# Stage B of an FFT mixer moved from block-diagonal 128x128 matmuls to 64x64 array tiles, inside a fused mixer and gated FFN

## The chip, the cores and the metric

One core of a Trainium2 chip runs the whole kernel. The metric is the device time of one execution in microseconds; lower is better. Engines are named as in the profile: PE (matmul), PEld (weight load), DVE (VectorE), ACT (ScalarE), POOL (GpSimd), SP (the queue that issues most DMAs).

## The reference

```python
def _attn_ref(x, filt_r, filt_i):              # x: (8, 3008, 256)
    X = np.fft.rfft(x, axis=1)
    Y = X * (filt_r + 1j * filt_i)[None]       # 1505 frequencies x 256 channels
    return np.fft.irfft(Y, n=x.shape[1], axis=1)

def _moe_ref(x, w_gate, w_val, w_out):         # x: (24064, 256), d_ff = 1536
    return (np.maximum(x @ w_gate, 0.0) * (x @ w_val)) @ w_out
```

The output of the first function, reshaped to 24064 rows, is the input of the second.

## The kernel before, in words

The transform of length 3008 is factored as 94 x 32. For each of the 8 batches there are three stages:

- **Stage A** is the transform of length 94. Batches 0 and 1 take it in `items_a`: 16 items, each one fp32 matmul of 128x96 weights `WA` on 512 columns of `XF`, a copy by ACT, and a write to the DRAM buffer `Abuf` after every fourth item. Batches 2 to 7 take `load_chunk`, `fold_chunk` and `tiled_a`, four chunks per batch: six DMAs bring `x` into a buffer `XP`, POOL folds it with six additions and subtractions, and sixteen fp32 matmuls on 32x32 array tiles transform it.
- **Stage B** (`items_b`) reads `Abuf` back transposed as `at`. The 94 frequencies of stage A are 48 lines, held as 24 groups of two. For two groups at a time, `fwd` makes the 32-point transform: two matmuls of 256 columns with weights `F2[:, g]` into one PSUM bank `psX`. DVE multiplies the bank twice, with the real and the imaginary filter, into `tt` and `uu`. `inv` makes the inverse 32-point transform: four matmuls with `I2t` and `I2u`, accumulating in `psD`, which ACT copies to `dsb`; a DMA writes it to `Dbuf`. The weights of a group are block-diagonal 128x128 matrices, one 64x64 block for each of its two lines; the other half is zero.
- **Stage C** (`item_c`) reads `Dbuf` as `dC` and makes the inverse of length 94 so that its output is the FFN input `yT`, 512 tokens at a time.

The FFN runs over 47 blocks of 512 tokens, and each block over 12 steps. A step is `gv` (two matmuls of 512 columns for `psV`, two for `psG`; ACT copies `psV` to `vsb`, DVE makes relu(gate) times value) and `o_part` of the block before (four matmuls of 256 columns). The order of work is written by hand: `at_step(s, f)` hangs pieces of stages A and B and their DMAs on step numbers, and `side` is emptied after each step's matmuls. `item_c` of the next block follows at steps 8 and 10 of each block. Stage B of batches 1 to 7 hangs on every second step, as 12 pieces of `fwd` and `inv` and two more of `inv`.

Before step 0 stands a prologue: stage A of batch 0, the making of `I2t` and `I2u` from `F2` (`make_back`), loading of the filters, stage B of batch 0 with dummy matmuls (`warm`) and three items of A of batch 1 in between (`amid`), the other 13 items, and `item_c` of block 0. Six products of batch 0 go to POOL instead of DVE (`POOL_G`), for which ACT first copies the bank to `xs`.

PSUM is four tags of two banks each: `fft`, `psv`, `psg`, `pso`. In the prologue stages rotate over all four; afterwards `fft_tag` gives `fft` alone, so that stages B and C share its two banks.

Of the kernel before, what the change touches and what calls it, by code (L numbers as in the profile page):

```python
# [30 lines left out]
NROW = 96  # L31
# [10 lines left out]
def _tables():  # L42
# [3 lines left out]
    wa = np.zeros((128, NROW + 2))  # L46
    for a in range(2):
        wa[64 * a:64 * a + 64, NROW + a] = 1.0
# [7 lines left out]
    for hg in range(48):  # L56
        g, a = divmod(hg, 2)
        rows = slice(a * 64, a * 64 + 64)
        f = np.zeros((64, 64))
# [4 lines left out]
        wa[part, 2 * hg] = np.cos(th)  # L64
        if k1 not in (0, 47):
            wa[part, 2 * hg + 1] = -np.sin(th)
            m1[48 * a + g] = 2.0 * np.cos(th) / S
            m1[48 * a + 24 + g] = -2.0 * np.sin(th) / S
# [8 lines left out]
        else:  # L77
            m1[48 * a + g] = np.cos(th) / S
# [15 lines left out]
        f2[lo + 64 * a, g] = f  # L94
# [4 lines left out]
    col = 4 * (8 * (r % 4) + r // 4 % 8) + 2 * (r // 64) + r // 32 % 2  # L99
    perm = np.zeros((128, 128))  # L100
    perm[r, col] = 1.0
# [15 lines left out]
    tab = np.concatenate([f2.reshape(128, -1), perm, swap, own.reshape(128, -1), m1], 1)  # L117
    return wa.astype(np.float32), fold.reshape(128, 128).astype(np.float32), tab.astype(NBF16)
# [3 lines left out]
def kernel(  # L122
# [17 lines left out]
    NZ = 8  # L140
# [4 lines left out]
    wa_h, fold_h, tab_h = _tables()  # L145
# [14 lines left out]
    WA = pro.tile([128, NROW + 2], FP32)  # L160
    WF = consts.tile([128, 4, 32], FP32)
    M1 = consts.tile([NROW, N1], BF16)
    F2 = consts.tile([128, NG, 128], BF16)
    I2t = consts.tile([128, NG, 128], BF16)
    I2u = consts.tile([128, NG, 128], BF16)
# [20 lines left out]
    f2c = tabs[:, 0:NG * 64].rearrange("p (g f) -> p g f", f=64)  # L186
    perm, swap = tabs[:, NG * 64:NG * 64 + 128], tabs[:, NG * 64 + 128:NG * 64 + 256]

    def place_forward():
        for a in range(2):  # L190
            nc.vector.tensor_scalar(F2[:, :, a * 64:a * 64 + 64], f2c,
                                    WA[:, NROW + a:NROW + a + 1], None, op0=ALU.mult)
        nc.vector.tensor_copy(M1, tabs[:NROW, NG * 64 + 512:])

    def make_back(i, q):

        psI = ps.tile([128, 4, 128], FP32, tag=fft_tag(), name="psI")
        gs = slice(4 * q, 4 * q + 4)
        if i == 0:
            for j in range(4):  # L200
                nc.tensor.matmul(psI[:, j], F2[:, 4 * q + j, :], perm, start=True, stop=True)
        else:
            nc.tensor.matmul(psI, swap, I2t[:, gs, :], start=True, stop=True)
        copy = nc.scalar.copy if i == 1 else nc.vector.tensor_copy
        copy((I2t, I2u)[i][:, gs, :], psI)

    def place_own():

        for i, t in enumerate((I2t, I2u)):
            o = NG * 64 + 256 + i * 128  # L210
            nc.vector.tensor_copy(
                t[64:, NG - 2:, :].rearrange("p g (n a c) -> p g n a c", a=2, c=2)[:, :, :, 1, :],
                tabs[64:, o:o + 128].rearrange("p (g n c) -> p g n c", g=2, c=2))
# [50 lines left out]
    def fft_tag():  # L264
        turn["i"] += 1
        return turn["tags"][turn["i"] % len(turn["tags"])]

    def items_a(b):

        def one(c, j, st):  # L270
            if j == 0:
                st["asb"] = sb.tile([128, NC2 * D], BF16, tag="asb", bufs=4, name="asb")
            psA = ps.tile([128, 512], FP32, tag=fft_tag(), name="psA")
            o = (c * NC2 % NX2) * D + j * 512
            nc.tensor.matmul(psA[0:NROW], WA[:, :NROW], XF[c * NC2 // NX2][:, o:o + 512],  # L275
# [13 lines left out]
    def load_chunk(b, j):  # L289

        xp = XP[(4 * b + j) % 3]
        for q in range(4):
            r, o = 32 * q, 8 * q + 2 * j
            nc.sync.dma_start(xp[r:r + 24, 0:4:2, :],
                              _ap(x, (b * N1 * N2 + o) * D,
                                  [[N2 * D, 24], [47 * N2 * D, 2], [1, 512]]))
        for i in range(2):
            nc.sync.dma_start(xp[:, 2 * i + 1, :],
                              _ap(x, ((b * N1 + 46 + 47 * i) * N2 + 2 * j) * D,
                                  [[8 * D, 4], [-N2 * D, 32], [1, 512]]))  # L300

    def fold_chunk(b, j):

        xp = XP[(4 * b + j) % 3]
# [29 lines left out]
    def load_at_tiled(b):  # L334

        ats[b] = sb.tile([128, NG, D], BF16, tag="at", bufs=1, name="at")
        for rr in range(4):
            for e in range(2):
                nc.sync.dma_start(ats[b][32 * rr:32 * rr + 32, e:NG:2, :],
                                  _ap(Abuf[b], (48 * (rr % 2) + 24 * e + 12 * (rr // 2)) * N2 * D,  # L340
                                      [[D, 32], [N2 * D, 12], [1, D]]))

    GC = 6
    POOL_G = (4, 6, 10, 12, 16, 18)
# [8 lines left out]
    def items_b(b, amid=None):  # L353

        held = []
        st = {}
        lag = 2 if b else 3
        cuts = (0, 6, 12, 18, 24) if b else (0, 6, 12, 18, 22, 24)

        def fwd(g):  # L360
            at = ats[b]
            psX = ps.tile([128, 2, D], FP32, tag=fft_tag(), name="psX")
            for i in range(2):
                nc.tensor.matmul(psX[:, i], F2[:, g + i, :], at[:, g + i, :], start=True, stop=True)  # L364
            tt = sb.tile([128, 2, D], BF16, tag="tt", bufs=4)
            uu = sb.tile([128, 2, D], BF16, tag="uu", bufs=4)
            nc.vector.tensor_tensor(tt, psX, Ftr[:, g:g + 2, :], op=ALU.mult)  # L367
            if b == 0 and g in POOL_G:
                xs = pro.tile([128, 2, D], FP32, tag="xs", bufs=2)
                nc.scalar.copy(xs, psX)  # L370
                nc.gpsimd.tensor_tensor(uu, xs, Fti[:, g:g + 2, :], op=ALU.mult)  # L371
            else:
                nc.vector.tensor_tensor(uu, psX, Fti[:, g:g + 2, :], op=ALU.mult)  # L373
            held.append((g, tt, uu))

        def inv():
            g, tt, uu = held.pop(0)
            if g in cuts:
                st["dsb"] = sb.tile([128, GC, D], BF16, tag="dsb", bufs=4, name="dsb")
                st["g"] = g  # L380
            psD = ps.tile([128, 2, D], FP32, tag=fft_tag(), name="psD")
            for i in range(2):
                nc.tensor.matmul(psD[:, i], I2t[:, g + i, :], tt[:, i], start=True, stop=False)  # L383
                nc.tensor.matmul(psD[:, i], I2u[:, g + i, :], uu[:, i], start=False, stop=True)  # L384
            o = g - st["g"]
            nc.scalar.copy(st["dsb"][:, o:o + 2, :], psD)  # L386
            if g + 2 in cuts:
                nc.sync.dma_start(_ap(Dbuf[b], st["g"] * D, [[NG * D, 128], [1, (o + 2) * D]]),
                                  st["dsb"][:, :o + 2, :])

        for g in range(0, NG, 2):
            def both(g=g):
                fwd(g)
                if amid:
                    amid(g // 2)
                if len(held) > lag:
                    inv()
            yield both
        for _ in range(lag):
            yield inv  # L400
# [3 lines left out]
    def load_d(b, z0=0, z1=NZ):  # L404
        for z in range(z0, z1):
            dC = sb.tile([NROW, 4, D], BF16, tag="dC", bufs=12)
            nc.sync.dma_start(dC, _ap(Dbuf[b], z * 4 * NROW * D,
# [225 lines left out]
```

## Time and profile before

| what | value |
|---|---|
| median of 3 runs | 913.89 us (913.39 to 914.81) |
| the profiled execution's own time | 913.1 us |
| its span, first to last instruction | 911.3 us |
| PE busy / DVE / ACT / POOL | 98% / 63% / 55% / 29% |
| mean granted PE clock | 0.995 |

The span runs from the first to the last instruction of the core; 1.8 us of the execution lie around it. "Busy" of PE counts pipelined matmuls until their modelled end, so spacing between the starts of matmuls says more than their durations: a matmul of 512 columns is listed with 379 ns and the next one starts 216 ns after it.

### The profile page before, as it was taken

The numbers are of one execution on the slowest core, as the hardware profiler recorded it, in microseconds if no ns is written. First come the engines' busy times: TensorE is split into PE (matmuls) and PEld (weight loads), VectorE is DVE, ScalarE is ACT, GpSimd is POOL, SyncE is SP. The second block draws the span as 40 slices with busy tenths as digits, with TensorE's granted clock in tenths as the row PEclk, the third lists the DMA queues.
The fourth block names the chain that finished last, engine by engine and source line by source line (L and its number), as shares of the span: only waits on it lengthen the run. The fifth ranks groups of instructions, "written<-read, shape, count | busy, mean of one in ns | idle before, by whom it ended". The sixth has DMA issues, their size and how long they took to land.

```text
span 911.3 us, 18044 instructions
## 1 busy us (share of the span) xinstructions
PE 896.0 (98%) x6602; PEld 545.7 (60%) x6602; DVE 578.0 (63%) x875; ACT 500.8 (55%) x893; POOL 262.4 (29%) x181
## 2 busy tenths in 40 slices
PE   8799999999999999999999999999999999999997
PEld 3445665666655666556655566556665566666665
DVE  3737766568655775657755587555865567655553
ACT  4675555555555555555555555555555555555552
POOL 4340174405451074400844017440355300000000
PEclk9899999999999999999999999999999999999999
DMA  9996336444355345452353433525446242231111
GB/s 254 256 252 143 116 122 166 111 90 138 122 153 105 82 150 139 119 117 84 129 168 94 115 111 118 165 76 121 115 134 166 65 106 66 85 78 36 36 31 51
DMA packets 106138, 109.04 MB, mean 120 GB/s; under 512 B 9794, under 2 KB 87362, under 8 KB 105410
## 3 DMA queue, kind: packets, MB, share of 16 engines
q1 hardware_dynamic: 101222, 103.77, 40.7%
q0 software_dynamic: 4512, 3.90, 2.8%
q8 instruction: 52, 0.85, 0.4%
q14 instruction: 36, 0.29, 0.1%
q10 hardware_dynamic: 316, 0.22, 0.1%
HBM read 61.94 MB, written 49.81 MB: 123 GB/s over the span
## 4 chain that ended last, share of the span: by engine, by line
PE 95%; DMA 3%; SPq 0%; ACT 0%; POOL 0%; DVE 0%; issue 0%; ACTq 0%; POOLq 0%
PE psV L445 27%; PE psG L445 27%; PE psO L464 26%; PE psF L321 3%; PE psA L275 3%; PE psY L429 2%; PE psD L383 2%; PE psD L384 2%; PE psX L364 2%; DMA XF<-in_x_dram 1%; DMA Abuf<-asb 1%; DMA at<-Abuf 0%; DMA out_dram<-osb 0%; SPq L178 0%; SPq L478 0%
## 5 line engine op out<-in xcount | busy, mean ns | idle before, releaser
L450 DVE SCALAR_TENSOR_TENSOR prod<-psG,vsb 128x512 bf16<-128x512 f32 x564 | 390.0, 692 | 274.6 <-ACT vsb L448 265.6
L448 ACT CAST vsb<-psV 128x512 bf16<-128x512 f32 x564 | 332.0, 589 | 244.7 <-PE psV L445 206.4
L445 PE MATMUL psV<-yT,WvT 128*128 128x512 bf16 x1128 | 335.9, 379 | 0.9 <-ACT yT L434 0.7
L464 PE MATMUL psO<-WoT,prod 128*128 128x256 bf16 x2256 | 336.4, 273 | 0.0
L445 PE MATMUL psG<-yT,WgT 128*128 128x512 bf16 x1128 | 335.3, 379 | 0.0
L464 PEld LDWEIGHTS <-prod 128*128 128x128 bf16 x2256 | 220.7, 98 | 143.4
L445 PEld LDWEIGHTS <-WgT 128*128 128x128 bf16 x1128 | 110.0, 98 | 133.8 <-issue 0.5
L307 POOL TENSOR_TENSOR fold<-XP 128x1024 f32<-128x1024 f32 x24 | 56.4, 2351 | 404.5 <-DMA out_dram<-osb 170.9
L445 PEld LDWEIGHTS <-WvT 128*128 128x128 bf16 x1128 | 102.3, 98 | 33.1 <-issue 20.9
L386 ACT CAST dsb<-psD 128x512 bf16<-128x512 f32 x96 | 55.9, 588 | 51.7 <-PE psD L384 50.0
L367 DVE TENSOR_TENSOR tt<-psX,Ftr 128x512 bf16<-128x512 f32 x96 | 65.2, 682 | 4.2 <-PE psX L364 4.2
L470 ACT COPY osb<-psO 128x512 f32<-128x512 f32 x92 | 53.9, 586 | 22.7 <-PE psO L464 20.3
L373 DVE TENSOR_TENSOR uu<-psX,Fti 128x512 bf16<-128x512 f32 x90 | 61.3, 681 | 0.0
L308 POOL TENSOR_TENSOR XP<-XP 128x1024 f32<-128x1024 f32 x24 | 56.4, 2349 | 1.9
L384 PE MATMUL psD<-uu,I2u 128*128 128x256 bf16 x192 | 47.6, 276 | 0.6 <-POOL uu L371 0.6
L383 PE MATMUL psD<-tt,I2t 128*128 128x256 bf16 x192 | 47.9, 276 | 0.0
L328 ACT CAST asb<-psF 128x512 bf16<-128x512 f32 x48 | 25.8, 589 | 32.5 <-PE psF L321 32.5
L328 DVE CAST asb<-psF 128x512 bf16<-128x512 f32 x48 | 30.9, 686 | 17.3 <-PE psF L321 14.5
L364 PE MATMUL psX<-at,F 128*128 128x256 bf16 x192 | 37.8, 281 | 3.9 <-DMA at<-Abuf 3.9
L436 DVE CAST yT<-psY 128x512 bf16<-128x512 f32 x47 | 32.0, 681 | 12.9 <-PE psY L429 12.9
L434 ACT CAST yT<-psY 128x512 bf16<-128x512 f32 x47 | 27.5, 586 | 22.7 <-PE psY L429 22.6
L429 PE MATMUL psY<-M,dC 96*128 96x94 bf16 (+18 forms) x604 | 37.5, 198 | 0.0
(64 smaller groups left out, 439.9 us busy)
## 6 DMA issues: line engine op xcount, KB each, us to landing
dC<-Dbuf SPq DMA_DIRECT2D x64, 192.0 KB
XP<-in_x_dram SPq DMA_DIRECT2D x48, 256.0 KB
Dbuf<-dsb SPq DMA_DIRECT2D x31, 384.0 KB
XP<-in_x_dram SPq DMA_DIRECT2D x96, 96.0 KB
Abuf<-asb SPq DMA_DIRECT2D x96, 96.0 KB
at<-Abuf SPq DMA_DIRECT2D x48, 192.0 KB
out_dram<-osb SPq DMA_DIRECT2D x70, 94.0 KB
XF<-in_x_dram SPq DMA_DIRECT2D x12, 256.0 KB
```

Source lines behind the costliest of these rows:

```text
L307: tt(t, xp[:, 0:2], xp[:, 2:4], op=ALU.add)
L308: tt(xp[:, 2:4], xp[:, 0:2], xp[:, 2:4], op=ALU.subtract)
L328: copy(asf[:, :, q, :], banks[q])
L364: nc.tensor.matmul(psX[:, i], F2[:, g + i, :], at[:, g + i, :], start=True, stop=True)
L367: nc.vector.tensor_tensor(tt, psX, Ftr[:, g:g + 2, :], op=ALU.mult)
L373: nc.vector.tensor_tensor(uu, psX, Fti[:, g:g + 2, :], op=ALU.mult)
L383: nc.tensor.matmul(psD[:, i], I2t[:, g + i, :], tt[:, i], start=True, stop=False)
L384: nc.tensor.matmul(psD[:, i], I2u[:, g + i, :], uu[:, i], start=False, stop=True)
L445: nc.tensor.matmul(pt[:, :W], w[:, h, ft * 128:(ft + 1) * 128], yt[:, h, :], start=(h == 0), stop=(h == 1))
L448: nc.scalar.copy(vsb, psV[:, :W])
L450: nc.vector.scalar_tensor_tensor(prod, in0=psG[:, :W], scalar=0.0, in1=vsb, op0=ALU.max, op1=ALU.mult)
L464: nc.tensor.matmul(psO[:, t % 2], prods[ft][:, t * 128:(t + 1) * 128], WoT[:, ft, :], start=(ft == 0), stop=(ft == NFT - 1))
```

## The change

Five things are done.

1. Stage B is issued on 64x64 array tiles. `fwd(b, i)` takes four groups at a time with eight matmuls of 64x64 weights (`tile_position=(64*e, 64*a)`), into two PSUM banks, one for each row half `e`. `inv(b, i)` takes sixteen matmuls into two banks `psD`. A batch needs six of each. `F2`, `I2t`, `I2u` hold 64 columns per group instead of 128, `F2` comes straight by DMA, and `make_back_t`/`make_back_u` are three calls each, of which the first uses 64x64 tiles too.
2. For batches 1 to 7 stage B stands at seven steps in place of fourteen, "excursions" here: the first has a `fwd`, five have a `fwd` and the `inv` of the excursion before, the last has an `inv`. The four products of an excursion stand on four steps in a row. `psX` takes both `fft` banks; `psD` takes one bank of `psv` and one of `psg`.
3. Stage B of batch 0 is six excursions; seven of its 24 products go to POOL. After excursion 2 one item of A of batch 1 follows, after each of 3, 4 and 5 two, in banks of `pso`; nine are left for afterwards. `x` of batch 1 is loaded in smaller first pieces.
4. The `x` chunks of batches 2 to 7 are loaded by POOL's queue, one per FFN block, each held until `yT` of the next block is being made; the folding of a chunk follows the load of the next.
5. `dC` tiles hold eight rows in place of four (half as many, two DMAs each), `load_at_tiled` takes four DMAs in place of eight, `XP` has four buffers, `osb` four in place of five, and `dsb` is written in three pieces for each batch in place of four.

```diff
-    for i in range(2):
-        nc.tensor.matmul(psX[:, i], F2[:, g + i, :], at[:, g + i, :], start=True, stop=True)
...
+def fwd(b, i):
+    for e in range(2):
+        psXs[b, i, e] = ps.tile([128, 2, D], FP32, tag=fft_tag(), name="psX")
+    for m in range(2):
+        for e in range(2):
+            for a in range(2):
+                j = 12 * a + 2 * i + m
+                nc.tensor.matmul(psXs[b, i, e][64 * a:64 * a + 64, m],
+                                 F2[64 * e:64 * e + 64, j, :],
+                                 ats[b][64 * e:64 * e + 64, j, :], start=True, stop=True,
+                                 tile_position=(64 * e, 64 * a))
...
+def product(b, i, e, k, pool=False):
+    psX = psXs[b, i, e]
...
+    if pool:
+        xs = pro.tile([128, 2, D], FP32, tag="xs", bufs=3)
+        nc.scalar.copy(xs, psX)
+        nc.gpsimd.tensor_tensor(p, xs, filt, op=ALU.mult)
+    else:
+        nc.vector.tensor_tensor(p, psX, filt, op=ALU.mult)
...
+def inv(b, i, tags=None, cuts=CUTS):
...
+    for m in range(2):
+        for k in range(2):
+            for a in range(2):
+                for e in range(2):
+                    nc.tensor.matmul(psD[a][64 * e:64 * e + 64, m],
+                                     (I2t, I2u)[k][64 * a:64 * a + 64, 4 * i + 2 * m + e, :],
+                                     tus[b, i, e, k][64 * a:64 * a + 64, m],
+                                     start=(k == 0), stop=(k == 1),
+                                     tile_position=(64 * a, 64 * e))
...
+def first_b(amid):
+    cuts = (0, 2, 4, 5, 6)
+    for i in range(6):
+        fwd(0, i)
+        if i > 1:
+            inv(0, i - 2, cuts=cuts)
+        for e in range(2):
+            product(0, i, e, 0)
+            product(0, i, e, 1, pool=(i, e) in POOL_U)
+        amid(i)
+    inv(0, 4, cuts=cuts)
+    inv(0, 5, cuts=cuts)
...
-        xp = XP[(4 * b + j) % 3]
+        xp = XP[j]
...
-            nc.sync.dma_start(xp[r:r + 24, 0:4:2, :],
+            nc.gpsimd.dma_start(xp[r:r + 24, 0:4:2, :],
...
-    load_x(1, nc.sync, WHOLE)
+    load_x(1, nc.sync, ((0, 0, 2 * q), (0, 2 * q, 4 * q), (1, 0, 4 * q)))
...
 def amid(i):
-    if i < 9:
-        warm(1, 128)
+    if i < 2:
+        warm(3, 256)
     else:
-        next(early)()
+        for _ in range(2 if i > 2 else 1):
+            next(early)()
...
-    load_d(0, 0, 2)
+    load_d(0, 0, 1)
...
-        sb0 = 19 if b == 1 else end - 30 | 1
...
+            for j, e in enumerate((-74, -69, -64, -57)):
+                l = end - 113 + NFT * j
+                def next_x(b=b, j=j, l=l):
+                    hold_gpsimd(yTs[l // NFT + 1][:, 0, 0:8])
+                    load_chunk(b, j)
+                    if j:
+                        fold_chunk(b, j - 1)
+                    if j == 3:
+                        fold_chunk(b, j)
+                at_step(l, next_x)
+                at_step(end + e, lambda b=b, j=j: tiled_a(b, j))
+            at_step(end + e + 4, lambda b=b: load_at_tiled(b))
+        for i, l in enumerate((-35, -28, -25, -22, -16, -11, -4) if b == 1 else
+                              (-40, -35, -28, -23, -16, -11, -4)):
+            if i < 6:
+                at_step(end + l, lambda b=b, i=i: fwd(b, i))
+                for h in range(4):
+                    at_step(end + l + h, lambda b=b, i=i, h=h: product(b, i, h // 2, h % 2))
+            if i > 0:
+                at_step(end + l, lambda b=b, i=i: inv(b, i - 1, ("psv", "psg")))
+        at_step(end - 2, lambda b=b: load_d(b))
```

Here `end` is `(b * S // W - 1) * NFT + C_AT[0] - 5`: step 51 for batch 1 and 72 steps more for each further batch.

## The prediction

> **What bounds it now.** First the page's busy times and the chain that ended last:
>
> ```profile
> PE 896.0 (98%) x6602; PEld 545.7 (60%) x6602; DVE 578.0 (63%) x875; ACT 500.8 (55%) x893; POOL 262.4 (29%) x181
> PE 95%; DMA 3%; SPq 0%; ACT 0%; POOL 0%; DVE 0%; issue 0%; ACTq 0%; POOLq 0%
> ```
>
> PE carries the chain. Busy shares overstate a pipelined engine, so next the PE timeline, where only starts count:
>
> ```profile
> 47.68 0.27 PE L383 MATMUL psD<-tt,I2t 128*128 128x256 bf16 x1
> 47.79 0.27 PE L384 MATMUL psD<-uu,I2u 128*128 128x256 bf16 x1
> 47.90 0.27 PE L383 MATMUL psD<-tt,I2t 128*128 128x256 bf16 x1
> ```
>
> Listed as 0.27 us, they start 0.11 apart (0.109 in the trace's records). Between 61.9 and 905.8 us I added up all starts: L445 keeps 0.216, L464 and stage B's L364, L383, L384 keep 0.109 all through, and the only losses are one start 0.63 us late at 73 us and the entries into and exits from L321. Hence in the FFN part **every matmul slot taken away is time**, and a wait only costs if PE feels it. An FFN step is 4 x 0.216 + 4 x 0.109 = 1.30 us.
>
> How array tiles behave is seen at `tiled_a`:
>
> ```profile
> 135.37 0.60 PE L464 MATMUL psO<-WoT,prod 128*128 128x256 bf16 x4
> 135.90 0.61 PE L321 MATMUL psF<-XP,WF 24*32 24x512 f32 x1
> ...
> 136.04 0.62 PE L321 MATMUL psF<-fold,WF 24*32 24x512 f32 x2
> ...
> 136.64 0.59 PE L321 MATMUL psF<-XP,WF 24*32 24x512 f32 x1
> 137.16 0.39 PE L445 MATMUL psV<-yT,WvT 128*128 128x512 bf16 x1
> ```
>
> and in the weight loads there:
>
> ```profile
> 136.06 0.11 PEld L321 LDWEIGHTS psF<-fold,WF 24*32 24x32 f32 x2
> ```
>
> The last L464 starts at 135.37 + 3 x 0.109 = 135.70 and L321 follows 0.20 later, 0.09 over its slot. After the last L321 (512 fp32 columns in two passes of 0.43, as L275 shows) PE goes on after 0.52, again 0.09 over. One pass of sixteen tiles to the next takes about 0.46, so tiles run side by side; and the load at 136.06 is for the second pass of tiles whose first pass started at 136.04, so a load hides under a running matmul of its own tile. The whole takes 1.26 us, of which 2 x 0.43 are work, 0.09 the exit and 0.31 a stagger: the third and fourth row start 0.13 and 0.27 late, behind semaphore instructions for their banks.
>
> Last, the prologue:
>
> ```profile
> 43.75 1.07 PE L275 MATMUL psA<-XF,WA 128*96 128x512 f32 x2 [1.54 <-DMA XF<-in_x_dram]
> 49.43 11.32 PE L275 MATMUL psA<-XF,WA 128*96 128x512 f32 x26
> 60.59 0.61 PE L429 MATMUL psY<-M,dC 96*128 96x94 bf16 x11
> 53.14 1.67 SPq L407 DMA_DIRECT2D dC<-Dbuf x2
> ```
>
> PE waits for `x` of batch 1 and then has 11 us of stage A before `psY`; but the second `dC` that `psY` needs lands only at about 60.4 us by its semaphore, so the DMA chain is as long as PE's.
>
> **What the Trainium skill says.** "TensorEngine Tiling (Array Packing)", Tiling Modes, Key Properties: a change of tiling mode drains the engine. The trace agrees, 0.09 in and 0.09 out. The same page, Tile-to-Partition Mapping, Restrictions: column tiling switches the fast weight load off. No 64-column bf16 load is in this trace. "TensorE: Matmul & The Clock Gate", Part 3, The mechanism: a load overlaps running matmuls only where its row group differs. The 136.06 row speaks against it; the measurement decides. "DMA: Bandwidth & Descriptors", Issuing engines are not separate DMA queues: another issuing engine saves only issue time; no run here shows it.
>
> **Stage B, batches 1 to 7.** Removed: per batch 24 matmuls of L364 and 48 of L383/L384, 72 x 0.109 = 7.85 us, 54.9 in all. Added: 48 + 96 matmuls on 64x64 tiles. Four tiles run side by side, so 36 packs of four; a pack of 256 columns is taken at 0.109, from L364. That gives 3.92 per batch, 27.5 in all. Mode changes: 7 excursions x 7 batches x 0.18 = 9.0. Waits inside an excursion: `fwd` and `inv` each open two banks, so the second half of the tiles starts behind its semaphore instruction; tiled_a's stagger of 0.31 is the ceiling, nothing (hidden behind running packs) the floor, and I take 0.15: 49 x 0.15 = 7.4. Sum 43.9 against 54.9, **-11.0**. A pack's own bounds are 0.109 and 0.13 (the 0.46 against 0.43 of a tiled_a pass, with room), up to +5.
>
> **DVE and ACT around it.** Products and `dsb` copies keep their number and shape. Backlogged products start 0.60 apart (34.59, 35.19, 35.79 for L373 and L367), so a step of STT (0.69) and one product costs DVE 1.30: it just keeps pace for four steps, and the excursion ahead of them (about 1 us without STT) gives slack. ACT gets two `psD` copies of 0.59 at once; the next `vsb` is then some 0.8 late, and the two buffers of `psv` and `psg` hide that, since they are needed again a step later. I cost both at nothing for batches 2 to 7, where excursions are five or more steps apart. **Batch 1** has them at steps 23, 26 and 29: the fourth product of one stands on the very step whose `fwd` wants its bank. There STT and that product (0.69 + 0.65) run while PE waits, with `gv` of the next step behind it: 1.35 x 2 = **+2.7**. Its `at` loads move from step 5 to 3 and the first `fwd` from 19 to 16; the last part landed at 77.9 us before, 1.7 us earlier now, and step 16's `fwd` stands near 80.
>
> **Queues.** Per chunk six DMAs go from SP to POOL. POOL then has, at the fourth chunk, six issues of about 0.6 (its other issues take 0.5 to 0.85) and two foldings of 9.8 (234.4 us over 24, L307 to L312): 23 us, against 20 steps of 1.30 and three tiled_a of 1.4, 30 us. Margin 7, cost nothing. The tiny hold waits for a `yT` that is already made. SP loses those 144 issues (L294, L298), some of which waited there for a free `XP` ahead of others, so `Dbuf`, `dC` and `at` can only go earlier; `load_d` at `end - 2` instead of `end - 3` waits for the `dsb` write anyway, and its first use is seven steps (9 us) away. Fewer DMAs for `at`, `dC`; one `osb` buffer less leaves four of about 8 us each. All nothing, covered by PE's 98%.
>
> **Prologue.** Placing F2 (two DVE operations of 1.15) goes, but DVE was idle 8.3 us before them. A of batch 0 keeps its length, six inserts of 0.25 becoming three of some 0.35. The dummy matmuls grow from 18 to 36 of 0.216, but with A's end at 24.1 and three matmuls of L203 they end near 32.5, and `at` still lands at 33.2. They close an idle stretch after which the granted clock was 0.64 to 0.68 (the view by windows, 30 to 40 us); stage B of batch 0 waits for DVE there, so that is worth 0.2 at most. DVE loses one of 18 products. What counts: item 0 of A now stands in PE's order before the fourth `fwd`, so DVE, after its eight products of excursions 0 to 2, waits for `x`. The first half piece is 0.77 MB; the first third of the old whole pieces (0.52 MB) landed at 38.8 and the second at 42.2, so I put it at 41.0. Then: A 0.86, `fwd` 0.4, two rounds of 2.5 (two A, `fwd`, `inv`), four products of 0.64, `inv` 0.5, two copies 1.2: the last `dsb` at about 51.7, where it was at 50.6. PE finishes A at 58 instead of 60.6, but `dC` goes through the same landing, issue and crowded load (7 us to the second) and lands near 61.4. **+0.8**, bounds -2.5 (`x` at 38, `dC` less crowded) and +2.5 (`x` at 42.5). The weights' second half, behind the same write, keeps its distance.
>
> **Sum.** -11.0 + 2.7 + 0.8 = -7.5 on the profiled execution's 913.1 us (span 911.3 and 1.8 around it): 905.6. The median stands 0.8 above that execution, so **906.4**. From no change a measurement here can tell about 0.2%, 1.8 us.
>
> **Rivals.** *Weight loads in series (slower).* "TensorE: Matmul & The Clock Gate", LDWEIGHTS, gives columns divided by 1.2 ns: an estimate of 53 ns for 64 columns. If the four loads of a pack queue behind each other, a pack is 0.213: 252 x 0.213 = 53.7, plus 9.0 + 7.4 + 2.7 + 0.8 = 73.6 against 54.9, +18.7: **932.6**. It decides from a pack of (54.9 - 19.9) / 252 = 0.139 on. Against it: tiled_a's loads start about 7 ns apart. For it: those are 32 columns wide with 0.43 us of cover each. *The whole gain:* semaphores hidden, one of the two stalls filled, `x` early: -18.4 + 1.35 - 1.5, **895.4**; PE's queue does run ahead of waits in the FFN steps. *POOL late:* chunk loads from POOL that take 9 us more than the margin, or landings as slow, let each batch's last tiled_a wait 1.5 us, 6 x 1.5 = 9: **915**, no change. Against it, a chunk with nothing ahead of it was folded 3 us after its last issue (205.0 to 208.0). That tiles do not run side by side at all is excluded by tiled_a.
>
> **Numbers.** Forecast 0.64, its own range 899 to 912; whole gain 0.13; POOL late 0.07; loads in series 0.16. Faster 0.77, within 0.2% 0.07, slower 0.16. The range takes the pack's and the semaphores' bounds and reaches from the whole gain to just above the third rival: 895 to 917.
>
> **What would show it.** Stage B's matmuls in packs of four 0.11 apart, 0.20 from L464 into the first and 0.2 out; an excursion with `fwd` and `inv` about 1.0 us. DVE idle from about 39 to 42 us, waiting for `psX`. PE idle for `dC` before `psY`. Two PE gaps of 1.3 at steps 26 and 29, none at tiled_a. Packs above 0.139, or gaps at tiled_a in every batch, would make it wrong.

## The result, and the profile after

The changed kernel takes 907.55 us (median of 4 runs, 905.93 to 907.86) against 913.64 (913.24 to 914.81) for the kernel before: ratio 0.9928, 95% interval 0.991 to 0.9945. The forecast was 906.4. The profiled execution took 907.27 us, its span is 905.5, the mean granted clock 0.995 as before. That looks like a forecast that came true. Summed stage by stage it is a gain much larger than forecast and a loss much larger than forecast, and the experiments are about both.

The page's busy times and the chain that ended last, kernel after:

```profile
PE 875.3 (97%) x7096; PEld 512.1 (57%) x7217; DVE 566.6 (63%) x872; ACT 498.6 (55%) x891; POOL 359.0 (40%) x351
PE 86%; DVE 4%; DMA 4%; ACT 3%; issue 1%; SPq 1%; POOL 0%; DVEq 0%; POOLq 0%
```

PE is still the bound, but its share of the chain fell from 95% to 86%: waits are back. (121 of 7217 matmuls have no record, which may be some of that fall too; the weight loads are complete, and steps below are counted by the loads of `WvT`.) Next the PE timeline of one excursion in the FFN part; columns are start, busy time, engine, line, operation:

```profile
215.59 0.60 PE L483 MATMUL psO<-WoT,prod 128*128 128x256 bf16 x4
216.12 0.41 PE L363 MATMUL psX<-at,F 64*64 64x256 bf16 x8
216.36 0.28 PE L393 MATMUL psD<-tt,I2t 64*64 64x256 bf16 x4
216.47 0.28 PE L393 MATMUL psD<-uu,I2u 64*64 64x256 bf16 x4
216.58 0.28 PE L393 MATMUL psD<-tt,I2t 64*64 64x256 bf16 x4
216.69 0.28 PE L393 MATMUL psD<-uu,I2u 64*64 64x256 bf16 x4
216.90 0.60 PE L464 MATMUL psV<-yT,WvT 128*128 128x512 bf16 x2
```

Each row of four is a pack, 0.11 after the one ahead of it, although every matmul brings its own weight load. The last L483 starts at 215.59 + 3 x 0.109 = 215.92 and L363 at 216.12, 0.20 later; the last pack starts at 216.69 and L464 0.21 later. So both mode changes cost 0.09 over a slot, as at `tiled_a` before. A step with `fwd` and `inv` takes 2.279 us and the one behind it 1.207, instead of 1.300 each: an excursion costs 0.886. Six packs are 0.654 of that, the mode changes 0.186, and only 0.046 is left for all waits inside. With 0.45 for a batch's first excursion and 0.67 for its last, stage B takes 5 x 0.886 + 1.12 = 5.55 us per batch instead of 7.85.

The losses are in the waits of PE between 60 and 130 us (in total, times, longest):

```profile
PE psG L464 <- DMA WgT<-in_moe_w_gate_dram: 2.5, 1, 2.5
PE psX L363 <- DVE uu L379: 2.2, 2, 1.1
PE psX L363 <- issue: 1.8, 1, 1.8
PE psY L448 <- DMA dC<-Dbuf: 1.1, 2, 0.7
```

and in the prologue's PE timeline:

```profile
42.11 1.99 PE L276 MATMUL psA<-XF,WA 128*96 128x512 f32 x2 [3.80 <-DMA XF<-in_x_dram]
44.03 0.64 PE L363 MATMUL psX<-at,F 64*64 64x256 bf16 x8
...
62.83 0.64 PE L448 MATMUL psY<-M,dC 96*128 96x94 bf16 x12 [0.39 <-DMA dC<-Dbuf]
63.90 0.72 PE L464 MATMUL psV<-yT,WvT 128*128 128x512 bf16 x2 [0.44 <-ACT yT L453]
...
72.64 0.60 PE L464 MATMUL psG<-yT,WgT 128*128 128x512 bf16 x2 [2.54 <-DMA WgT<-in_moe_w_gate_dram]
```

The first `psV` is 2.0 us later than before (61.91). Inside block 0 PE then waits 2.54 us for the second half of the weights and 0.74 for a `dC`; block 1 begins at 78.55 where it began at 72.51, **+6.04**. At step 16 the first `fwd` of batch 1 waits for `at`, and the step is 1.86 us longer for it. ACT's timeline has the last four copies of `psD` to `dsb`, which end at 56.20 where the last one ended at 50.64 before:

```profile
54.15 2.05 ACT L400 CAST dsb<-psD 128x512 bf16<-128x512 f32 x4
```

Where the time went, from the starts of steps in the two traces:

| stretch | before | after | difference |
|---|---|---|---|
| up to step 0 | 61.03 | 63.28 | +2.25 |
| steps 0 to 12 (block 0) | 11.48 | 15.27 | +3.79 |
| steps 12 to 24 (`at` of batch 1) | 17.73 | 19.93 | +2.20 |
| steps 24 to 36 (products of batch 1) | 19.99 | 21.47 | +1.48 |
| steps 36 to 486 (the later excursions and every `tiled_a`) | 685.7 | 669.8 | -15.9 |
| later steps | the same | the same | 0.0 |

One execution stands for each kernel here. How far that carries can be seen from the profiles of five runs below whose edit does not touch the prologue (*split*, *tile_by_tile*, *b1_early*, *sp_queue*, *b2_late*): up to step 0 they take 62.6 to 63.4 us, and block 0 takes 14.5 to 16.0.

### The profile page after: what moved, and what is told of

Same layout as the page of the kernel before. It is cut to its first block, busy times and chain, and to the rows that moved or that the text cites. A ratio compares the mean times of both kernels' runs of the same rounds, so it can differ in the third digit from the quotient of the medians.

```text
span 905.5 us, 19111 instructions
## 1 busy us (share of the span) xinstructions
PE 875.3 (97%) x7096; PEld 512.1 (57%) x7217; DVE 566.6 (63%) x872; ACT 498.6 (55%) x891; POOL 359.0 (40%) x351
## 4 chain that ended last, share of the span: by engine, by line
PE 86%; DVE 4%; DMA 4%; ACT 3%; issue 1%; SPq 1%; POOL 0%; DVEq 0%; POOLq 0%
PE psG L464 25%; PE psO L483 25%; PE psV L464 24%; DVE prod L469 4%; PE psA L276 3%; PE psF L322 3%; ACT vsb L467 3%; PE psD L393 2%; PE psX L363 2%; PE psY L448 1%; DMA XF<-in_x_dram 1%; DMA dC<-Dbuf 1%; DMA Abuf<-asb 1%; DMA out_dram<-osb 0%; DMA at<-Abuf 0%
## 5 line engine op out<-in xcount | busy, mean ns | idle before, releaser
L483 PE MATMUL psO<-WoT,prod 128*128 128x256 bf16 x2256 | 336.6, 273 | 1.5
L464 PE MATMUL psG<-yT,WgT 128*128 128x512 bf16 x1099 | 329.1, 379 | 7.4 <-DMA WgT<-in_moe_w_gate_dram 2.5
L464 PE MATMUL psV<-yT,WvT 128*128 128x512 bf16 x1037 | 316.9, 380 | 0.7 <-ACT yT L453 0.4
L483 PEld LDWEIGHTS <-prod 128*128 128x128 bf16 x2256 | 220.7, 98 | 143.4
L464 PEld LDWEIGHTS <-WgT 128*128 128x128 bf16 x1128 | 109.9, 98 | 136.9 <-DMA WgT<-in_moe_w_gate_dram 3.0
L464 PEld LDWEIGHTS <-WvT 128*128 128x128 bf16 x1128 | 98.1, 98 | 41.8 <-issue 30.4
L258 POOL CAST scr<-yT 128x8 f32<-128x8 bf16 x24 | 4.6, 191 | 265.8 <-ACT yT L453 265.8
L400 ACT CAST dsb<-psD 128x512 bf16<-128x512 f32 x96 | 51.5, 589 | 28.5 <-PE psD L393 28.4
L295 POOL DMA_DIRECT2D XP<-in_x_dram x96 | 56.4, 592 | 0.9 <-issue 0.5
L448 PEld LDWEIGHTS <-dC 96*128 96x128 bf16 x604 | 34.5, 97 | 4.6 <-DMA dC<-Dbuf 1.2
```

What stands on the lines that cost most here:

```text
L295: nc.gpsimd.dma_start(xp[r:r + 24, 0:4:2, :], _ap(x, (b * N1 * N2 + o) * D, [[N2 * D, 24], [47 * N2 * D, 2], [1, 512]]))
L400: nc.scalar.copy(dsb[:, a, o:o + 2, :], psD[a])
L448: nc.tensor.matmul(psY[:, o:o + w], dCs[b, n2 // 8][:, n2 % 8, h * 128:(h + 1) * 128], M1[:, n1:n1 + w], start=True, stop=True)
L464: nc.tensor.matmul(pt[:, :W], w[:, h, ft * 128:(ft + 1) * 128], yt[:, h, :], start=(h == 0), stop=(h == 1))
L483: nc.tensor.matmul(psO[:, t % 2], prods[ft][:, t * 128:(t + 1) * 128], WoT[:, ft, :], start=(ft == 0), stop=(ft == NFT - 1))
```

## The experiments

All times are medians of runs beside runs of the kernel before on the same chip; the ratio is to that kernel, and the changed kernel's own is 0.9928. One hundredth of ratio is 9.1 us.

### What an excursion costs

**split.** `inv` one step after its `fwd`, so that 35 excursions are each cut in two.

```diff
-                at_step(end + l, lambda b=b, i=i: inv(b, i - 1, ("psv", "psg")))
+                at_step(end + l + (i < 6), lambda b=b, i=i: inv(b, i - 1, ("psv", "psg")))
```

> The changed kernel with the inv of excursions 1 to 5 of each batch moved one step after its fwd, 35 more changes of tiling mode and no other work. Theory (a mode change costs 0.093 in and 0.093 out, and the stagger at an opening of banks 0.02 to 0.05): 35 x (0.19 to 0.23) = +6.5 to +8.1 us, so 914.1 to 915.7. Rival (an excursion's overhead is mostly waiting for banks, and the drain is covered by them): under +3 us.

Measured: 914.98 us, ratio 1.0013 (1.0 to 1.0025). The PE timeline of a split excursion:

```profile
197.08 0.60 PE L483 MATMUL psO<-WoT,prod 128*128 128x256 bf16 x4
197.61 0.41 PE L363 MATMUL psX<-at,F 64*64 64x256 bf16 x8
197.96 0.61 PE L464 MATMUL psV<-yT,WvT 128*128 128x512 bf16 x2
...
198.83 0.60 PE L483 MATMUL psO<-WoT,prod 128*128 128x256 bf16 x4
199.36 0.30 PE L393 MATMUL psD<-tt,I2t 64*64 64x256 bf16 x4
```

The same gap of 0.20 stands ahead of L363 and once more ahead of L393 (199.36 against 198.83 + 0.33). From step 54 to step 486 the trace is 6.69 us longer, 1.115 per batch, 0.22 for each of the five added entries and exits. The price of a mode change is thereby measured apart from the packs. Since 35 x 0.22 = 7.8 us is more than the whole measured gain of the change, grouping `fwd` with `inv` is not a detail of this kernel: with the same tiles and each `inv` on a step of its own the change would have brought nothing.

**tile_by_tile.** The same matmuls in another order: all of one tile's ahead of the next tile's, so that matmuls next to each other in the program want the same tile.

```diff
-        for m in range(2):
-            for k in range(2):
-                for a in range(2):
-                    for e in range(2):
+        for a in range(2):
+            for e in range(2):
+                for m in range(2):
+                    for k in range(2):
```

`fwd` likewise (`e` and `a` outside, `m` inside).

> The changed kernel with the same 64x64 matmuls issued tile by tile (loops over a and e outside, m and k inside) instead of round the four tiles. Theory (matmuls start in program order, so four run side by side only if neighbours in the order name different tiles): a fwd takes 0.53 us in place of 0.21 and an inv 1.39 in place of 0.43, 1.28 us more per pair, 42 pairs in batches 1 to 7: about +50 us, 950 to 965. Rival (the array takes a later matmul for a free tile ahead of a waiting one): no change, 906 to 909.

Measured: 908.77 us, ratio 0.9945 (0.9927 to 0.9963), no difference that can be told from the changed kernel. The PE timeline:

```profile
215.74 0.42 PE L363 MATMUL psX<-at,F 64*64 64x256 bf16 x8
215.99 0.33 PE L393 MATMUL psD<-tt,I2t 64*64 64x256 bf16 x4
216.09 0.33 PE L393 MATMUL psD<-uu,I2u 64*64 64x256 bf16 x4
...
```

In the program a `tt` matmul of a tile is followed by the `uu` matmul of the same tile; on the chip four `tt` matmuls start, and 0.11 later four `uu`, then the same again at 216.20 and 216.31. That the order in the queue did change shows in the spacing: the four starts of the first `tt` pack lie within 0.033 us instead of 0.010. The step takes 2.325 us instead of 2.279. So a matmul whose tile is free starts ahead of one that stands earlier in the program and whose tile is busy, and the packs don't hang on the order that the kernel writes. The theory fell by 50 us. The Trainium skill, "TensorE: Matmul & The Clock Gate", Part 3, The mechanism, lists that matmuls are not reordered and that a load overlaps only where its row group differs; the paragraph above that list also lets a load run ahead into a background weight buffer. This run contradicts the first for matmuls on different tiles. The excursion above contradicts the second as it is listed, and would fit the buffer: at 216.25 the loads for its third pack start, 0.002 us after the second pack has started on the same four tiles.

### The products of batch 1

**b1_early.** The fourth product of batch 1's second and third excursion stands one step earlier, beside the third.

```diff
-                    at_step(end + l + h, lambda b=b, i=i, h=h: product(b, i, h // 2, h % 2))
+                    at_step(end + l + (min(h, 2) if b == 1 and i in (1, 2) else h),
+                            lambda b=b, i=i, h=h: product(b, i, h // 2, h % 2))
```

> The changed kernel with the fourth product of batch 1's excursions 1 and 2 one step earlier, so that it no longer stands on the step whose fwd wants its bank. Theory (those products cause the two late fwd at steps 26 and 29, 1.42 and 1.33 us over the 2.28 of the other such steps): -2 to -2.7 us, 905 to 905.6. Rival (DVE has no room for two products in one step and the stall moves to psG a step or two later): 0 to -1 us.

Measured: 906.53 us, ratio 0.9915 (0.9899 to 0.9931), an interval that overlaps the changed kernel's, so that the traces have to decide. In the changed kernel's PE timeline the stall stands inside a `fwd`:

```profile
102.49 0.30 PE L363 MATMUL psX<-at,F 64*64 64x256 bf16 x2
103.92 0.41 PE L363 MATMUL psX<-at,F 64*64 64x256 bf16 x6 [1.13 <-DVE uu L379]
```

Steps 26 and 29 take 3.70 and 3.61 us instead of 2.28; with the edit 3.10 and 3.01. It takes 0.6 from each, not 1.4: DVE has the product one step earlier in its queue, but needs about 1.3 us for a step of STT (its relu(gate) times value) and one product, so it is still behind when the `fwd` comes, and PE still waits for it twice, 0.5 us each time instead of 1.1. The cause was right, the cure is half of one.

### The queues and batch 1's `at`

**sp_queue.** The `x` chunks back on SP's queue, everything else as changed (a chunk's other DMA likewise).

```diff
-            nc.gpsimd.dma_start(xp[r:r + 24, 0:4:2, :],
+            nc.sync.dma_start(xp[r:r + 24, 0:4:2, :],
```

> The changed kernel with one part undone: the x chunks are loaded by SP's queue again, at the same steps. Theory (PE's slots decide, queues are covered): same time within 1 us of the changed kernel's 907.6, so 906.6 to 908.6 or a ratio to before of 0.992 to 0.994; POOL loses about 85 us of DMA issues. Rival (the move to POOL's queue is what brought the gain, by freeing SP): 2 us slower or more, with gaps at tiled_a or late dC.

Measured: 909.17 us, ratio 0.9949 (0.9932 to 0.9966), outside the theory's range and just short of the rival's 2 us; the interval overlaps the changed kernel's. The trace shows two differences of one size: the wait for `at` at step 16 is gone (steps 12 to 24: -1.86 us), and steps 36 to 486 are 1.86 us longer. The second is the late `dC` that the rival named, at steps 56, 272 and 344; the changed kernel has no such wait there:

```profile
PE psY L448 <- DMA dC<-Dbuf: 1.7, 3, 0.9
```

The move between queues did not make the gain. Whether it keeps `dC` from being late in general, one execution does not show.

**b2_late.** The call that loads the first chunk of batch 2 moves from step 10 to step 18.

```diff
-                at_step(l, next_x)
+                at_step(l + (8 if b == 2 and j == 0 else 0), next_x)
```

> The changed kernel with the first x chunk of batch 2 loaded at step 18 instead of 10. Theory (it is in flight beside at of batch 1, whose last part lands at 87.5 where the fwd at step 16 has waited 1.8 us for it): that wait goes, -1 to -2 us, 905.5 to 906.5. Rival (at is late because Abuf and the weights are, not because of the chunk): no change within 0.7 us.

Measured: 905.81 us, ratio 0.9915 (0.9902 to 0.9929), an interval that overlaps the changed kernel's. The wait at step 16 falls from 1.8 us to 0.3, which looks like the theory. But the edit did not move the transfer. POOL's timeline, of the changed kernel and of this one:

```profile
77.01 2.40 POOL L295 DMA_DIRECT2D XP<-in_x_dram  x4
```

```profile
76.70 2.39 POOL L295 DMA_DIRECT2D XP<-in_x_dram  x4
```

Step 18 begins only at 87.36 here. A step number places a call in POOL's order of work; POOL has nothing else between the two places, and what lets it go on is the hold in `next_x`, which in both kernels waits for `yT` of block 1. So the shorter wait is not the work of the edit, and the theory was not tested. The wait for `at` at step 16 differs between executions anyway: in profiles in which this chunk stands at the same place it is absent (*keep_clock*, *w2_free*), 1.6 to 1.8 (*w_late*, the changed kernel), or 3.8 and 4.4 (*b1_early*, *a_late*). In the changed kernel the chunk's six DMAs are issued from 77.0 to 80.8 us, while `at` of batch 1 is under way, whose last part lands at 87.54; that the two transfers hold each other up is possible and not shown. The profiled runs of *b1_early* and *a_late* I read by their other stretches.

### The prologue

**w_late.** The first half of the FFN weights, issued ahead of `x` of batch 1, is issued after it.

```diff
-    load_vg(0, DFF // 2)
     nc.sync.dma_start(gate, ats[0][0:32, NG - 1, 0:8])
...
+        if i == 2:
+            load_vg(0, DFF // 2)
```

> The changed kernel with the first half of the FFN weights issued by POOL after the products of excursion 2 of batch 0 instead of ahead of x of batch 1. Theory (x shares the DMA engines with them, lands at 42.0 and holds A's first item, then DVE, dsb, dC, the second weights and at of batch 1 in a row): the first piece lands near 38, psV of block 0 starts 3 to 5 us earlier (63.9 before this edit), the 2.5 us wait for WgT goes, in all -5 to -8 us, 900 to 903. Rival (A's items in B's order are what delays it, whatever lands when; or the weights then arrive late at block 0): -1 us to +3 us.

Measured: 904.08 us, ratio 0.9886 (0.9873 to 0.9899). Its PE timeline:

```profile
39.47 1.99 PE L276 MATMUL psA<-XF,WA 128*96 128x512 f32 x2 [1.29 <-DMA XF<-in_x_dram]
...
61.40 0.72 PE L464 MATMUL psV<-yT,WvT 128*128 128x512 bf16 x2 [0.44 <-ACT yT L453]
```

`x` lands at 39.34 us instead of 41.97 and `psV` starts at 61.40 instead of 63.90. 2.6 us of `x` are 2.5 us of `psV`, three times the spread of the unedited prologues: the prologue hangs on this transfer. The wait for `WgT` does not go but grows, from 2.54 to 3.07, so that the total falls by 3.8 us (by the ratios) and not by the 5 to 8 of the theory.

**before_w_late.** The same edit in the kernel before.

> The kernel before, with only the first half of the FFN weights issued after x of batch 1 (at the end of the fourth piece of its stage A in between) instead of ahead of it. Theory: that x lands late costs time only where stage A stands ahead of the last excursions, as in the changed kernel; in the kernel before stage B of batch 0 does not wait for x, dC sets psY, and the edit gives less than 1 us: ratio 0.999 to 1.001. Rival: the weights crowd the transfers of Dbuf and dC in either kernel, and the edit gives about 3 us here too: ratio near 0.9965.

Measured: 913.21 us, ratio 0.9994 (0.9985 to 1.0002). In its trace `x` is early too: it has landed at 42.07 instead of 43.62, and the wait of 1.54 us for it is gone. There that is worth nothing that can be told, so the landing of `x` became dear only through the new order, in which stage A stands ahead of half of the excursions.

**keep_clock.** In the changed kernel the first item of stage A takes twice its time. The view by windows shows why; the columns are the stretch, its length, busy time (instructions) of PE, PEld, DVE, ACT and POOL, the granted PE clock, the DMA share and GB/s:

```profile
40.00:42.00 2.00, 0.00 (x0) 0.00 (x0) 0.00 (x0) 0.37 (x1) 2.00 (x2) 0.57 1.06 335
42.00:44.00 2.00, 1.89 (x2) 0.39 (x2) 0.00 (x0) 0.00 (x0) 0.22 (x1) 0.50 1.08 337
44.00:46.00 2.00, 2.00 (x26) 1.30 (x26) 1.29 (x3) 1.02 (x2) 0.00 (x0) 0.50 1.17 425
```

While PE idles for `x` (3.80 us) the granted clock falls to 0.50, at about 40.3 us by the 0.57 of the first row, and it stays there until about 47.1, for the first work after the wait. The Trainium skill, "TensorE: Matmul & The Clock Gate", Part 1, What's actually happening, puts it so: an idle window of about 3.4 us halves the clock until the array has been busy for about as long. The trace agrees on the size, 0.50 for 6.8 us or two such windows. It does not agree that the window has to be idle: PE's last matmuls before the fall had started at 37.8 to 38.0, in the 3.4 us ahead of it. Nor does it take the long wait for `x`. In *w_late* the item took 1.99 us too, after a wait of 1.29, and in *a_late* below it does so after one of 0.24:

```profile
42.69 1.99 PE L276 MATMUL psA<-XF,WA 128*96 128x512 f32 x2 [0.24 <-DMA XF<-in_x_dram]
```

PE had stood still for products between 36 and 38 us as well, and which of its pauses costs the clock is not separated here. The edit fills the wait with dummy matmuls:

```diff
         else:
+            if i == 2:
+                warm(16)
```

> The changed kernel with sixteen dummy matmuls of 512 columns (16 x 0.216 = 3.5 us) after the third excursion of the first stage B, in the stretch from 38.3 to 42.1 us in which TensorE idles for x of batch 1. In the changed kernel's profile the granted clock is 0.50 from 42 to 46 us and 0.72 from 46 to 48, and the work there takes twice its time (the first item of stage A 1.99 us instead of 1.07). Theory: the idle stretch costs the clock, so that with it filled the first item, the fourth fwd, the inv beside it and the next two items take 0.9 + 0.2 + 0.4 + 0.8 us less; the last dsb copy, psV and what follows stand 1.5 to 2.3 us earlier: about 905.5 us, ratio to the kernel before 0.990 to 0.9915. Rival: the clock falls anyway, since TensorE had also idled for the products between 36 and 38 us, or dC's landing takes back what the products gain: within 0.7 us of the changed kernel, ratio 0.992 to 0.9935.

Measured: 904.53 us, ratio 0.9893 (0.9876 to 0.9909). The same view of this kernel:

```profile
40.00:42.00 2.00, 2.00 (x10) 0.80 (x8) 0.00 (x0) 0.65 (x2) 1.76 (x2) 0.84 1.08 337
42.00:44.00 2.00, 2.00 (x12) 0.69 (x11) 0.00 (x0) 0.00 (x0) 0.50 (x1) 1.00 1.08 338
```

The clock falls all the same, as the rival said, here at about 37 us, so that the dummies take 4.6 us instead of 3.5 and stage A starts 0.9 later, at 43.02. But with PE kept busy the clock is back at about 40.6 (the 0.84 of the first row), and the slow stretch lies under the wait. The item takes 1.02 us instead of 1.99, and the fifth `fwd` follows the fourth after 2.67 instead of 4.12. The last `dsb` copy ends 1.3 us earlier and step 0 stands 1.75 earlier. The theory held in what the slow clock costs, not in that filling the wait would keep it up. The total is 3.2 us below the changed kernel's by the ratios, more than 1.75; in the trace the wait for `at` at step 16, which differs between executions, is gone too (-1.86), and block 0 is 1.19 longer, as `WgT` is late all the same (PE waits 3.1 for it).

**a_late.** No item of stage A after excursion 2; one after 3, two after 4 and 5, eleven afterwards.

```diff
-        if i < 2:
+        if i < 3:
...
-            for _ in range(2 if i > 2 else 1):
+            for _ in range(2 if i > 3 else 1):
```

> The changed kernel with no item of A of batch 1 after excursion 2 of batch 0; one after 3, two after 4 and 5, eleven afterwards. x lands as before. Theory (A's first item stands in PE's order ahead of the fourth fwd and holds DVE and with it dsb, dC and the second weights; x lands late because of the first weights): fwd 3 moves from 44.0 to about 38.6, the last dsb from 56.2 to 52.5, psV of block 0 from 63.9 to about 62, the wait for WgT from 2.5 to about 0.5: -3 to -5 us, 902.5 to 904.5. Rival (DMA arrival alone decides the prologue, and DVE idles later instead): 0 to -1 us.

Measured: 904.1 us, ratio 0.9888 (0.9872 to 0.9903). The total falls by 3.7 us by the ratios, as the theory said. Step 0 stands 2.28 us earlier than in the changed kernel, block 1 3.4 us. (The longer wait for `at` of this execution lies later and is left out of this.) The fourth `fwd` no longer stands behind `x`, so products and `dsb` come earlier, and `Dbuf` is written at 55.97 instead of 58.64. The order of A in between is thus one of the causes, and it is largely the same loss as that of *w_late*, met from the other end: *best_a* and *best_b* below show that the two gains don't add.

**w2_free.** Here the second half of the weights no longer waits for batch 0's `Dbuf`: the tiny read `last` that holds POOL's queue is taken out.

```diff
-    nc.gpsimd.dma_start(pro.tile([1, D], BF16, tag="last", bufs=1, name="last"),
-                        _ap(Dbuf[0], (N2 * NROW - 1) * D, [[D, 1], [1, D]]))
```

> The changed kernel without the small read of Dbuf that holds the second half of the FFN weights and w_out behind batch 0's last dsb write. Theory (the write is 5.6 us later than before the change, so WgT lands after block 0 wants it): the issue moves from 59.5 to about 52, the wait of 2.5 us for WgT goes, dC may land up to 2 us later: -1 to -3 us, 904.5 to 906.5. Rival (dC, crowded by the weights, takes the time back): -0.5 to +2 us.

Measured: 909.47 us, ratio 0.9952 (0.994 to 0.9965). The weights are there at 61.55 us and the wait for `WgT` is gone, but SP's and PE's timelines show what they pushed aside:

```profile
52.70 3.94 SPq L402 DMA_DIRECT2D Dbuf<-dsb  x3
65.14 0.84 SPq L425 DMA_DIRECT2D dC<-Dbuf  x2
```

```profile
69.19 1.04 PE L448 MATMUL psY<-M,dC 96*128 96x94 bf16 x12 [6.84 <-DMA dC<-Dbuf]
```

The same three `Dbuf` writes, issued at the same time, land up to 65.0 us instead of 58.6, and `psY` waits 6.84 us for `dC`. The theory fell, the rival held: by the ratios the kernel is about 2 us slower than the changed one, though the two intervals just meet, so the hold costs no more than it saves.

### Together

**best_b** is *w_late*, *b2_late* and *b1_early*; **best_a** is these and *a_late*. Of the three edits in *best_b* only two act, since that of *b2_late* moves no transfer: POOL issues the chunk at 76.10 and 73.34 us in the two kernels, as before right after `yT` of block 1.

> The changed kernel with three edits that each took time off alone: the first half of the FFN weights issued after x of batch 1, batch 2's first x chunk eight steps later, and the fourth product of batch 1's second and third excursion one step earlier. Theory: they act in three different places (the prologue up to psV; the wait for at at step 16; the waits at steps 26 and 29), so that their gains add: about -3 -1.5 -1.2, some 901.5 us, ratio to the kernel before 0.985 to 0.988. Rival: the three share one cause (what the DMA engines carry between 35 and 90 us) and the second gain is then already contained in the first: 903.5 to 904.5, ratio 0.989 to 0.990.

> The same three edits and, on top, stage A of batch 1 begun only after the fourth excursion of the first stage B. Theory: with x landed earlier, stage A in between still holds up the products and so the last dsb copy, and moving it behind frees some 1 to 2 us more up to psV: 899.5 to 900.5 us. Rival: once x is early, PE has nothing to wait for and the order of stage A and the excursions no longer matters, since the landing of Dbuf and dC sets psV either way: within 0.7 us of the kernel without this edit.

Measured: best_b 902.41 us, ratio 0.9871 (0.9856 to 0.9886); best_a 902.31 us, ratio 0.9878 (0.986 to 0.9895). *best_b* is 5.2 us below the changed kernel by the ratios, where *w_late* and *b1_early* alone gave 3.8 and 1.2. Both kernels are faster than the changed kernel, and the two can't be told apart: the rival of *best_a* held. In the profiled execution of *best_a* PE's share of the chain is nearly that of the kernel before again:

```profile
PE 94%; DMA 3%; DVE 1%; ACT 1%; issue 0%; POOL 0%; SPq 0%; DVEq 0%; ACTq 0%
```

Its span is 898.8 us, 6.7 below the changed kernel's: 2.57 up to step 0, 1.11 in block 0, 1.64 in steps 12 to 24 and 1.20 in steps 24 to 36, which is 6.5; the 1.64 is the wait for `at`, which differs between executions. In best_b's profiled execution step 0 stands no earlier than in the changed kernel, because `psY` waits 4.7 us for `dC`; its gain comes from the later stretches. That transfer is what still varies in the prologue, and it wasn't followed further.

## Why the prediction was right, and where it was wrong

The time was right to 0.13%, and that was luck as much as skill: a gain mis-sized by 5.7 us and losses mis-sized by 7.1 cancelled for the most part. The terms of its sum beside what the traces show:

| term | predicted | measured |
|---|---|---|
| stage B, batches 1 to 7 | -11.0 | -16.1, and -0.6 at `tiled_a` |
| products of batch 1 | +2.7 | +2.75 |
| `at` of batch 1 | 0 | +1.86 |
| prologue, up to step 0 | +0.8 | +2.25 |
| block 0 | 0 | +3.79 |
| sum | -7.5 | -6.1 |

Two sums of the forecast are 0.2 off, without weight for the result: 49 x 0.18 is 8.8 and not 9.0, and the terms up to the last `dsb` add up to 51.5 and not 51.7. The measured sum is that of the steps; the span fell by 5.8, as 0.35 us came back after the last step.

**Packs and mode changes** were right, 0.109 for a pack and 0.09 in and out. This excludes the rival with weight loads in series, which wanted packs of 0.213. Both numbers had been read from rows of the kernel before (L364's slot, `tiled_a`'s gaps).

**Waits inside an excursion** were mis-sized: 0.15 taken, 0.046 measured. 49 x 0.104 = 5.1 us is the whole difference of the first row. The value was borrowed from `tiled_a`'s stagger, the nearest row, and halved; the floor of nothing, which the prediction also gave, was the better end. The prediction put that stagger down to semaphore instructions, and did not ask whether an excursion would have any. The traces show how closely the time goes with them. A `tiled_a` with two semaphore instructions of their own between its rows of tiles takes 1.25 to 1.40 us, with one 1.17 or 1.18, with none 1.07; this holds for all 48 of both traces. The six with none are the first of each batch in the changed kernel, without an edit in them. Of the 49 excursions none has such an instruction between its tiles: where its matmuls wait, they carry the wait themselves. The six short `tiled_a` make 1.1 us, of which others that became longer took back 0.5.

**Products of batch 1**: step 26 and 29, 1.42 and 1.33 over, predicted 1.35 each. Counting DVE's work on the very step whose `fwd` wants the bank was enough.

**`at` of batch 1** was costed at nothing because its load moves up by two steps; in the profiled execution it cost 1.86. The prediction counted the issue and not the landing. Why the last part lands late is open: the wait ran from nothing to 4.4 us between executions, and no edit here moved the neighbouring chunk by itself.

**The prologue** came to +2.25 up to step 0, inside its bounds of -2.5 to +2.5 but near their end. The mechanism was named (DVE waits for `x`; the `dC` chain bounds `psY`), the size was not. Along its own chain: `x` at 41.0, measured 41.97; the fourth `fwd` at 41.9, measured 44.03; the sixth at 46.9, measured 50.81; the last `dsb` at 51.7, measured 56.2. Of these 4.5 us 1.0 is `x`; about 2.4 is the half clock, in the first item of A and in the round up to the fifth `fwd` (1.0 and 1.45 by *keep_clock*); about 0.6 is at the end, where the last four `dsb` copies stand behind copies of stage A on ACT. The prediction had the clock in hand, and valued it at 0.2 us, since in the kernel before the slow stretch, from about 31.8 to 38.6 us by the same view, lay where PE waits for DVE. It did not ask where the slow stretch would go: from 40.3 to 47.1, onto stage A and the excursions that the last `dsb` hangs on.

**"The weights' second half keeps its distance"**, a term put at nothing, is the step that failed. Block 0 came to +3.79, 2.54 of it this wait. The second half was issued 5.6 us later (60.22 instead of 54.61), behind the `Dbuf` write, and took 12.4 us to land instead of 9.9, at 72.59; PE wanted it at 70.1. A distance is only kept when it is written as a landing and a need, and neither number was in the text. *w2_free* shows that the wait can't simply be dropped: with the weights early, `dC` is late. Nor does it help to bring `Dbuf` forward alone: in *w_late* and *keep_clock* step 0 comes forward as well, and the wait is 3.1. In *best_a* 0.9 us of it is left.

**The rivals.** The whole gain came nearly true inside stage B, -16.1 of its -18.4, and not in the total. POOL late didn't show: no wait of PE stands at `tiled_a`. What ate the gain was none of the three but the prologue and block 0: +6.04 together, where +0.8 was taken and the bounds were -2.5 and +2.5.

## What to carry to other kernels

Price array tiles by packs, entries and exits, and put all tiled work into as few excursions as PSUM has banks for: here 35 more entries and exits would have cost all that the change gained. When work is reordered so that PE will wait, ask where the granted clock is low and what will stand there, and write every transfer that is "moved along" as a landing against a need. A forecast that hits the total should still be taken apart by stage: here the experiments found 5 us more in terms that had cancelled. And before an experiment is read, its trace should show that the edit moved what it was meant to move: *b2_late* gave the time that was forecast and had moved nothing.

## What was not expected of the hardware

- Matmuls on different tiles run side by side whatever their order in the program: with each tile's matmuls written one after the other the packs stayed 0.11 us apart, and a step took 2.325 us instead of 2.279.
- A load of 64 columns hides under running matmuls of 256 columns on its own tile: packs stand at 0.109 us, the same as untiled matmuls of 256 columns, with one load for every matmul.
- One more entry and exit of the tiled mode costs 0.22 us in all (0.09 in, 0.09 out, the rest not placed).
- The time of a `tiled_a` pass of 32x32 tiles goes with the number of separate semaphore instructions between its rows: 1.07 us without one, 1.17 or 1.18 with one, 1.25 and more with two. An excursion, whose matmuls carry their waits, has 0.046 us for all of them.
- The granted clock was 0.50 for 6.8 us behind a stretch in which PE was not quite idle, and cost about 2.4 us of work. Sixteen dummy matmuls did not keep it up, but it was back after 3.4 us, and step 0 came 1.75 us earlier.
